# Late rows of batches 4 to 7 computed between the output tiles, in a sliding-window attention and spectral-mixing kernel on Trainium2

## The chip, the cores and the metric

One NeuronCore of a Trainium2 chip runs the whole program. The metric is the device time of one execution in microseconds (us), as the median of several executions. Profiles come from single executions taken by the hardware profiler; their time axis starts with the span. PE is TensorE (PEld its weight loads), DVE is VectorE, ACT is ScalarE, POOL is GpSimd, and SP is SyncE, which here issues all the large DMAs.

## What is computed

```python
B, H, S, D = 8, 8, 576, 64          # batch, heads, sequence, head dim; DM = H * D = 512
scores = q @ k^T / sqrt(D) - slope[h] * |i - j|       # only 0 <= i - j < 128
x = softmax(scores) @ v              # as [B, S, DM]
X = rfft(x, axis=1)[:, :64]          # 64 modes
Y[m] = X[m] @ (w_r[m] + 1j * w_i[m]) # each mode its own 512x512 complex weight
y = irfft(Y, n=S)
u = x + y
out = u + relu(u @ w_ch)             # float32, [8, 576, 512]
```

The 64 modes' weights are 134 MB in float32, and they are most of what the program reads.

## The kernel before

The program has three stages. First, attention for 32 units (batch x pair of heads). Second, a product for each pair of modes (`_modes`, L687 to L729): the weights stream from HBM into a ring in SBUF, PE multiplies, and the results collect, transposed, in `ZT`. While the weights stream, PE also prepares the output: for each of the 36 output tiles (128 rows x 512) `_xw` (L749) forms x @ w_ch, plus x itself for all tiles that are not in `RELU`, and keeps it as two bf16 halves in `hl`. Third, the end stage, `_finish` (L848), which this change is about.

What is left at the end is the inverse transform. `Z[b]` holds Y of batch b with the 128 real and imaginary mode rows on the partitions, `ZW[b]` the same times w_ch. Most rows of both are made early (`_z_early`, L768). The last 32 rows of each batch, the late rows, need the last modes, and so the last weights. `_z_late` (L799) makes them for four batches at once: 16 products (`_z_product`, L786) on PE into one PSUM bank, each giving 32 partitions (columns 32c of the array, for c = 0 to 3, and four contraction steps `et`), and one copy into a bf16 tile `zl`. There are two banks for each four batches: w = 1 is ZW (`zlw`, moving operand 512 wide, accumulated over `et`) and w = 0 is Z (`zlp`, a transpose by the identity, 128 wide). `_z_put` (L813) moves 32 rows of `zl` into Z or ZW on GpSimd, 16 moves in all.

Each output tile is a PSUM bank `u` (`_known`, L831; six banks in turn). It takes the pair of `hl` halves (L745), then ZW's part by `_taken(.., 1)` (L825), which makes it x + x @ w_ch + y @ w_ch, or without x for tiles in `RELU`. Then `_greater` (L840) forms max(u, x) on DVE (L845), or for tiles in `RELU` relu(u) on ACT (L843). Next, `_taken(.., 0)` adds y. Tiles in `RELU` also get x by one more pair of matmuls just before that. At last ACT copies the bank to SBUF (L881) and SP issues the store (L886 for whole tiles, L889 as two halves for the four tiles that hold the last 64 rows of two batches: 8, 17, 26 and 31). Each of these terms is a pair of matmuls, one for each 64-column half of the array. With h = x @ w_ch + y @ w_ch, max(x + h, x) + y and relu(h) + x + y are the same value, x + y + relu((x + y) @ w_ch).

The order in the program is written out by hand, and each engine runs its instructions in that order. Before: both banks of batches 0 to 3 (L858, L859), the ZW bank of batches 4 to 7 (L860), then the first five tiles' late terms and their max (L861 to L863), with the Z bank of batches 4 to 7 behind tile 1 (L865), all 16 puts (L866 to L870), and then the loop over tiles (L871): the last term of tile i, the start of tile i+4, the copy of tile i, the max of tile i+4, and the store of tile i. So a max is asked for four tiles ahead of the tile's last term. Output buffers (`o`) are 16.

Of the kernel before, what the change touches and what calls it, by code (L numbers as in the profile page):

```python
# [9 lines left out]
FP32 = mybir.dt.float32  # L10
BF16 = mybir.dt.bfloat16
# [5 lines left out]
P = 128  # L17
# [15 lines left out]
FT_ROWS = (2, 3, 4, 5, 6)  # L33
FT_ORDERS = (10, 14, 18, 22)
WCH_ROWS = (1, 4)
RELU = (8, 16, 24, 32)
LAST = (0, 3, 5, 6)


# [5 lines left out]
def kernel(  # L45
# [52 lines left out]
    with tc.manual_schedule(engines={ET.SP, ET.PE, ET.Activation, ET.DVE, ET.Pool}):  # L98
        with ExitStack() as wctx:
# [129 lines left out]
            for m0, w in rest_w:  # L229
# [4 lines left out]
                if done in KNOWN_AT:  # L234
# [3 lines left out]
                    known = KNOWN_AT[done]  # L238
            mctx.close()
        _finish(g)  # L240


# [499 lines left out]
def _pair(nc, out, lhsT, rhs, **kw):  # L742

    for h in range(2):
        nc.tensor.matmul(  # L745
            out[64 * h : 64 * h + 64], lhsT=lhsT[h], rhs=rhs[h], tile_position=(0, 64 * h), **kw)


def _xw(g, n, xT, psum):  # L749
# [4 lines left out]
    xw = psum.tile([P, g.DM], FP32, tag="xw", bufs=2, name="xw")  # L754
    if n not in RELU:
        nc.tensor.matmul(xw, lhsT=g.ident_b, rhs=x, start=True, stop=False)
    for dt in range(4):
        nc.tensor.matmul(  # L758
            xw, lhsT=xT[:, dt], rhs=g.wch[:, dt],
            start=(dt == 0 and n in RELU), stop=(dt == 3))  # L760
    for h in range(2):
# [24 lines left out]
def _z_product(g, ps, w, et, k, l):  # L786

    ks = slice(32 * k, 32 * k + 32)
    if w:
        g.nc.tensor.matmul(  # L790
            ps[ks], lhsT=l, rhs=g.wch[:, et], start=(et == 0), stop=(et == 3),
            tile_position=(0, 32 * k))
    else:
        g.nc.tensor.matmul(
            ps[ks, et], lhsT=l, rhs=g.ident_b, start=True, stop=True,
            tile_position=(0, 32 * k))


def _z_late(g, b0, w, pool, tag, copy):  # L799


    ps = g.eps.tile([P, 4, P], FP32, tag="zp", name="zlp") if w == 0 else (
        pool.tile([P, g.DM], FP32, tag=tag, name="zlw"))
    for et in range(4):
        for c in range(4):
            l = g.ZT[:, et, 3].rearrange("p a m b -> p (a m) b")[:, :, b0 + c]
            _z_product(g, ps, w, et, c, l)
    t = g.fin.tile([P, g.DM], BF16, tag=f"zl{w}", bufs=2, name=f"zl{w}")
    copy(t, ps if w else ps.rearrange("p a b -> p (a b)"))
    g.late[w, b0] = t  # L810


def _z_put(g, w, b):  # L813

    ks = slice(32 * (b % 4), 32 * (b % 4) + 32)
    g.nc.gpsimd.tensor_copy((g.Z, g.ZW)[w][b][ks], g.late[w, b // 4 * 4][ks])


def _taken(g, i, w, late=None):

    rows = slice(0, 32) if late else slice(0, P)
    for h, (b, s) in enumerate(g.seq[i][1]):
        o = slice(32 * (b % 4), 32 * (b % 4) + 32) if late else rows
        z = late if late else (g.Z, g.ZW)[w][b]
        g.nc.tensor.matmul(  # L825
            g.u[i][64 * h : 64 * h + 64], lhsT=g.FT[o, b % 4, s : s + 64], rhs=z[o],
            start=False, stop=(w == 0 or late is not None or i >= KNOWN),
            tile_position=(o.start, 64 * h), skip_group_check=(w == 0))


def _known(g, i):  # L831

    pool, tag = ((g.fps, "f0"), (g.fps, "f1"), (g.lps, "l0"), (g.lps, "l1"), (g.lps, "l2"),
                 (g.kps, "k0"))[i % 6]
    g.u[i] = pool.tile([P, g.DM], FP32, tag=tag, name="u")
    _pair(g.nc, g.u[i], [g.ident2] * 2, [g.hl[:, i, h] for h in range(2)],
          start=True, stop=False)


def _greater(g, i):  # L840

    if i in RELU:
        g.nc.scalar.activation(g.u[i], g.u[i], AF.Relu)  # L843
    else:
        g.nc.vector.tensor_tensor(out=g.u[i], in0=g.u[i], in1=g.seq[i][0], op=ALU.max)  # L845


def _finish(g):  # L848

    nc, tc = g.nc, g.tc
    N = len(g.seq)
    with ExitStack() as fctx:
        g.fin = pool = fctx.enter_context(tc.tile_pool(name="fin", bufs=16))
        g.kps = fctx.enter_context(
            tc.tile_pool(name="kps", bufs=1, space=bass.MemoryType.PSUM, side="right"))
        _z_late(g, 0, 1, g.eps, "zwp", nc.scalar.copy)  # L858
        _z_late(g, 0, 0, g.eps, "zp", nc.vector.tensor_copy)  # L859
        _z_late(g, 4, 1, g.kps, "k0", nc.scalar.copy)  # L860
        for i in range(KNOWN):  # L861
            _taken(g, i, 1, g.late[1, 0])
            _greater(g, i)  # L863
            if i == 1:
                _z_late(g, 4, 0, g.eps, "zp", nc.scalar.copy)  # L865
        for w, b in ((0, 0), (1, 1), (0, 1), (1, 0), (1, 2), (0, 2), (1, 3), (0, 3)):  # L866
            _z_put(g, w, b)
        for b in range(4, 8):
            for w in (1, 0):
                _z_put(g, w, b)  # L870
        for i in range(N):  # L871
            x, n = g.seq[i][0], i + AHEAD
            if i in RELU:
                _pair(nc, g.u[i], [g.ident_b[:, 0:64], g.ident_b[:, 64:128]], [x] * 2,
                      start=False, stop=True, skip_group_check=True)
            _taken(g, i, 0)
            if KNOWN <= n < N:
                _known(g, n)
                _taken(g, n, 1)
            o = pool.tile([P, g.DM], FP32, tag="o", name="o")  # L880
            nc.scalar.copy(o, g.u[i])  # L881
            if KNOWN <= n < N:
                _greater(g, n)
            _, (lo, hi) = g.seq[i]
            if hi == (lo[0], lo[1] + 64):
                nc.sync.dma_start(out=g.out[lo[0], lo[1] : lo[1] + P], in_=o)  # L886
            else:
                for h, (b, s) in enumerate((lo, hi)):
                    nc.sync.dma_start(out=g.out[b, s : s + 64], in_=o[64 * h : 64 * h + 64])  # L889
# [30 lines left out]
```

## Time and profile before

| what | value |
|---|---|
| median of 3 runs | 449.3 us (448.2 to 451.52) |
| profiled execution | 450.29 us |
| its span | 448.5 us |
| mean granted TensorE clock | 0.769 of full speed; 1.00 from 391.9 to 443.1 |
| last weights in, last product of the modes | 414.2 us |
| first late product (zlw) | 414.86 us |
| first store issued | 419.55 us |
| last copy to SBUF ends | 442.27 us |
| output | 36 tiles, 40 stores, 9.44 MB |

Some groups of the end stage, 414 to 449, with count, busy us and mean ns of one:

| line, engine, what | count | busy | mean ns |
|---|---|---|---|
| L881 ACT copy o<-u 128x512 | 36 | 19.8 | 591 |
| L845 DVE max u<-u,x 128x512 | 32 | 21.0 | 697 to 700 |
| L843 ACT relu 128x512 | 4 | 2.3 | 582 |
| L816 POOL put 32x512 | 16 | 9.5 | 607 |
| L809 ACT copy zl 128x512 | 3 | 1.8 | 585 |
| L809 DVE copy zl 128x512 | 1 | 0.7 | 692 |
| L790 PE zlw 128x512 | 32 | 2.1 | 387 |
| L794 PE zlp 128x128 | 32 | 0.9 | 230 |

A row of a timeline has the start, the time that it covers, the engine, the line, the operation, out<-in, for PE the rows and columns of the array in use (128*64 is 128 rows, 64 columns), the shape, and the count of instructions merged into the row. A matmul's row covers its latency; the next matmul starts before it is over, so starts are what to compare. A table of stretches has busy us and count for each engine, the granted clock, the mean busy share of the core's 16 DMA engines, and the GB/s that they moved. For SP, a store's row is the time to issue it; its packets move later.

### The profile page before, as it was taken

To read this page: it belongs to the slowest core of one execution; us is meant where nothing else is said; L and a number is where in the kernel's file an instruction comes from. 1 tells how busy PE (TensorE), PEld (TensorE's weight loads), DVE (VectorE), ACT (ScalarE), POOL (GpSimd) and SP (SyncE) were. 2 spreads that over 40 slices of the span, in tenths; PEclk is the share of its full clock that TensorE was granted. 3 is DMA by queue.
4 is the path that set the end of the run, shared out by engine and by line. 5 is a ranking of instruction groups with operands and counts; after the bars stand their busy time and mean duration, and the time that the engine had idled before them with its cause. 6 is when DMAs were issued, how large, how long until landed. Compare 5 with 4: busy or idle time off the path is not lost.

```text
span 448.5 us, 12893 instructions
## 1 busy us (share of the span) xinstructions
PE 294.1 (66%) x5506; PEld 204.2 (46%) x5527; DVE 216.1 (48%) x427; ACT 189.6 (42%) x302; POOL 139.1 (31%) x257
## 2 busy tenths in 40 slices
PE   2467989887787885222235664854856748696993
PEld 2455767666666763111123333432433334464661
DVE  8458566566765661010002543453535345462882
ACT  3787656584866741000011331322313233251794
POOL 7699889586876702020000000000000000000700
PEclk9969576686988975555555988589778587899997
DMA  8999999999999999999999999999999999996498
GB/s 249 346 335 327 388 325 353 347 390 379 392 368 375 393 415 429 432 425 426 430 427 433 426 429 429 427 430 426 430 429 430 426 429 430 427 428 282 185 374 288
DMA packets 51562, 173.86 MB, mean 388 GB/s; under 512 B 4912, under 2 KB 21296, under 8 KB 43440
## 3 DMA queue, kind: packets, MB, share of 16 engines
q1 hardware_dynamic: 51120, 171.99, 97.2%
q0 software_dynamic: 384, 1.05, 0.9%
q8 instruction: 43, 0.70, 0.6%
q14 instruction: 15, 0.12, 0.1%
HBM read 163.58 MB, written 9.44 MB: 386 GB/s over the span
## 4 chain that ended last, share of the span: by engine, by line
DMA 50%; PE 26%; ACT 10%; DVE 6%; issue 4%; POOL 2%; ACTq 0%; POOLq 0%
DMA ring<-in_moe_w_r_dram 47%; ACT att L459 6%; PE acc L704 5%; PE sc L447 4%; PE xt L539 4%; PE u L825 3%; PE av L493 3%; DMA ring<-in_moe_w_i_dram 3%; ACT qkT L428 3%; PE tqk L420 2%; PE u L745 2%; POOL qkb L397 1%; PE xw L758 1%; DVE x_sb L507 1%; ACT mask L311 1%
## 5 line engine op out<-in xcount | busy, mean ns | idle before, releaser
L704 PE MATMUL acc<-Xz,ring 128*128 128x32 bf16 x2048 | 70.7, 183 | 100.2 <-DMA ring<-in_moe_w_r_dram 51.0
L704 PEld LDWEIGHTS <-ring 128*128 128x128 bf16 x2048 | 61.3, 101 | 130.1 <-DMA ring<-in_moe_w_r_dram 65.1
L763 ACT CAST hl<-xw 64x512 bf16<-64x512 f32 x72 | 41.7, 579 | 105.6 <-PE xw L758 70.9
L459 ACT ACTIVATE att<-sc 128x1024 bf16<-128x1024 f32 x64 | 65.6, 1025 | 32.8 <-PE sc L447 26.7
L764 DVE TENSOR_TENSOR hl<-xw,hl 64x512 bf16<-64x512 f32 x72 | 49.6, 688 | 58.1 <-ACT hl L763 57.8
L409 POOL CAST vb<-v 64x256 bf16<-64x256 f32 x128 | 64.7, 505 | 20.1 <-PE av L493 13.7
L783 POOL MEMSET ZTa<- 32x512 bf16 x2 | 1.0, 515 | 187.5 <-ACT ZTa L781 187.5
L447 PE MATMUL sc<-qkT,qkT 64*64 64x256 bf16 (+1 forms) x512 | 32.4, 330 | 30.1 <-ACT qkT L428 16.3
L758 PE MATMUL xw<-wch,xT 128*128 128x512 bf16 x138 | 46.3, 467 | 2.7 <-issue 2.2
L428 ACT COPY qkT<-tqk 128x576 bf16<-128x576 bf16 x64 | 40.7, 638 | 0.6 <-PE tqk L420 0.6
L420 PE MATMUL tqk<-ident_b,qkb 64*64 64x64 bf16 x1152 | 31.7, 214 | 7.6 <-POOL qkb L397 6.9
L420 PEld LDWEIGHTS <-qkb 64*64 64x64 bf16 x1152 | 30.8, 130 | 10.2 <-POOL qkb L397 9.2
L464 DVE TENSOR_TENSOR att<-att,mask 128x1024 bf16<-128x1024 bf16 x32 | 26.9, 839 | 14.7 <-ACT att L459 14.5
L585 ACT ACTIVATE Xz<-xz 128x192 bf16<-128x192 f32 (+1 forms) x24 | 7.5, 313 | 59.0 <-DVE Xz L584 57.9
L493 PE MATMUL av<-vb,att 128*128 128x65 bf16 (+1 forms) x512 | 30.8, 215 | 0.6 <-issue 0.2
L584 DVE CAST Xz<-xz 128x384 bf16<-128x384 f32 (+1 forms) x24 | 12.0, 511 | 36.4 <-PE xz L578 35.7
L447 PEld LDWEIGHTS <-qkT 64*64 64x64 bf16 x512 | 13.1, 120 | 35.3 <-ACT qkT L428 18.8
L397 POOL CAST qkb<-k 128x576 bf16<-128x576 f32 x32 | 27.5, 859 | 0.0
L493 PEld LDWEIGHTS <-att 128*128 128x128 bf16 (+1 forms) x512 | 24.4, 111 | 6.5 <-issue 0.6
L397 POOL CAST qkb<-q 128x576 bf16<-128x576 f32 x32 | 24.6, 768 | 6.1 <-PE tqk L420 3.3
L738 DVE COPY xT<-tp 128x512 bf16<-128x512 bf16 x36 | 15.2, 421 | 21.9 <-PE tp L736 21.4
L469 DVE TENSOR_TENSOR att<-att,mask 128x1024 bf16<-128x1024 bf16 x32 | 25.0, 780 | 1.5 <-ACT att L459 1.1
(104 smaller groups left out, 395.2 us busy)
## 6 DMA issues: line engine op xcount, KB each, us to landing
ring<-in_moe_w_r_dram SPq DMA_DIRECT2D x32, 1536.0 KB, 13.8
ring<-in_moe_w_i_dram SPq DMA_DIRECT2D x31, 1536.0 KB, 13.7
ring<-in_moe_w_i_dram SPq DMA_DIRECT2D x33, 512.0 KB, 8.0
ring<-in_moe_w_r_dram SPq DMA_DIRECT2D x32, 512.0 KB, 7.4
q<-in_q_dram SPq DMA_DIRECT2D x32, 288.0 KB, 6.3
k<-in_k_dram SPq DMA_DIRECT2D x32, 288.0 KB, 6.2
v<-in_v_dram SPq DMA_DIRECT2D x64, 128.0 KB, 5.8
out_dram<-o SPq DMA_DIRECT2D x32, 256.0 KB, 3.3
```

Source lines behind the costliest of these rows:

```text
L397: g.nc.gpsimd.tensor_copy(tb, t)
L409: g.nc.gpsimd.tensor_copy(o[64 * r : 64 * r + 64, i], v[64 * i : 64 * i + 64, r])
L420: g.nc.tensor.transpose(tp[hs, r, :], u.b[w][hs, r], g.ident_b[hs, hs], tile_position=(64 * hh, 64 * hh))
L428: g.nc.scalar.copy(dst.rearrange("c (p r) -> c p r", r=g.R), u.tp[w].rearrange("c r p -> c p r"))
L447: nc.tensor.matmul(sc[64 * r : 64 * r + 64, hh, 256 * i : 256 * i + nq], lhsT=kT[hs, c * P + r : c * P + P : 2], rhs=qT[hs, c * P : c * P ...
L459: nc.scalar.activation(a, sc, AF.Exp, scale=1.0 / math.sqrt(g.D))
L464: nc.vector.tensor_tensor(out=a, in0=a, in1=m, op=ALU.mult)
L493: nc.tensor.matmul(av[o, hh, col(t)], lhsT=att[c // 2][:, hh, q0 : q0 + m], rhs=u.vb[:, 2 * c + hh, 0 : D + 1], start=(j == 0), stop=(t < ...
L704: nc.tensor.matmul(acc[:, et, :, m0 - c0 : m0 - c0 + n, :], lhsT=wt[:, a, et * P : (et + 1) * P], rhs=X[:, a, 1 - w : 3 - w, m0 % MB : m0 ...
L758: nc.tensor.matmul(xw, lhsT=xT[:, dt], rhs=g.wch[:, dt], start=(dt == 0 and n in RELU), stop=(dt == 3))
L763: nc.scalar.copy(g.hl[own, n, h], xw[own])
L764: nc.vector.tensor_tensor(out=g.hl[other, n, h], in0=xw[own], in1=g.hl[own, n, h], op=ALU.subtract)
```

## The change

The late rows of batches 4 to 7 are taken out of the front of the end stage. The ZW bank's 16 products go in four groups of four behind tiles 3, 5, 7 and 9 of the loop, and its copy, now on DVE, behind the last group. The Z bank's 16 products and its copy (DVE instead of ACT) follow behind tile 11. The puts of batches 4 to 7 follow these copies, ZW of batch 4 first. The ZW bank of batches 4 to 7 uses the bank `zwp` instead of `k0`.

The first copy, ZW of batches 0 to 3, is cut in two halves of 256 columns, one on ACT and one on DVE. The Z copy of batches 0 to 3 goes from DVE to ACT.

The tiles in `RELU` are 8, 13, 15, 24 and 32 instead of 8, 16, 24 and 32: `_xw` leaves out the x term for tiles 13 and 15 and forms it for 16, and in the end stage tiles 13 and 15 have their relu on ACT and one more pair of matmuls.

```diff
-RELU = (8, 16, 24, 32)
+RELU = (8, 13, 15, 24, 32)
+ZW_LATE = (3, 5, 7, 9)
+Z_LATE = 11
...
-def _z_late(g, b0, w, pool, tag, copy):
-    ps = g.eps.tile([P, 4, P], FP32, tag="zp", name="zlp") if w == 0 else (
-        pool.tile([P, g.DM], FP32, tag=tag, name="zlw"))
-    for et in range(4):
+def _z_late(g, b0, w, ets):
+    if ets[0] == 0:
+        g.lp = g.eps.tile([P, 4, P], FP32, tag="zp", name="zlp") if w == 0 else (
+            g.eps.tile([P, g.DM], FP32, tag="zwp", name="zlw"))
+    for et in ets:
         for c in range(4):
             l = g.ZT[:, et, 3].rearrange("p a m b -> p (a m) b")[:, :, b0 + c]
-            _z_product(g, ps, w, et, c, l)
-    t = g.fin.tile([P, g.DM], BF16, tag=f"zl{w}", bufs=2, name=f"zl{w}")
-    copy(t, ps if w else ps.rearrange("p a b -> p (a b)"))
-    g.late[w, b0] = t
+            _z_product(g, g.lp, w, et, c, l)
+
+def _z_copy(g, b0, w, *copies):
+    src = g.lp if w else g.lp.rearrange("p a b -> p (a b)")
+    g.late[w, b0] = t = g.fin.tile([P, g.DM], BF16, tag=f"zl{w}", bufs=2, name=f"zl{w}")
+    n = g.DM // len(copies)
+    for i, copy in enumerate(copies):
+        copy(t[:, i * n : (i + 1) * n], src[:, i * n : (i + 1) * n])
...
-        _z_late(g, 0, 1, g.eps, "zwp", nc.scalar.copy)
-        _z_late(g, 0, 0, g.eps, "zp", nc.vector.tensor_copy)
-        _z_late(g, 4, 1, g.kps, "k0", nc.scalar.copy)
+        _z_late(g, 0, 1, range(4))
+        _z_copy(g, 0, 1, nc.scalar.copy, nc.vector.tensor_copy)
+        _z_late(g, 0, 0, range(4))
+        _z_copy(g, 0, 0, nc.scalar.copy)
         for i in range(KNOWN):
             _taken(g, i, 1, g.late[1, 0])
             _greater(g, i)
-            if i == 1:
-                _z_late(g, 4, 0, g.eps, "zp", nc.scalar.copy)
         for w, b in ((0, 0), (1, 1), (0, 1), (1, 0), (1, 2), (0, 2), (1, 3), (0, 3)):
             _z_put(g, w, b)
-        for b in range(4, 8):
-            for w in (1, 0):
-                _z_put(g, w, b)
         for i in range(N):
...
             if KNOWN <= n < N:
                 _known(g, n)
                 _taken(g, n, 1)
+            if i in ZW_LATE:
+                _z_late(g, 4, 1, [ZW_LATE.index(i)])
+            if i == ZW_LATE[-1]:
+                _z_copy(g, 4, 1, nc.vector.tensor_copy)
+                _z_put(g, 1, 4)
+            if i == Z_LATE:
+                _z_late(g, 4, 0, range(4))
+                _z_copy(g, 4, 0, nc.vector.tensor_copy)
+                for w, b in ((0, 4), (1, 5), (0, 5), (1, 6), (0, 6), (1, 7), (0, 7)):
+                    _z_put(g, w, b)
             o = pool.tile([P, g.DM], FP32, tag="o", name="o")
             nc.scalar.copy(o, g.u[i])
```

## The prediction

> **What bounds the kernel now.** I read the page first: its chain of waits is DMA for half of the span (the weight stream), and the weights' last packet is in at about 414. All that the change touches lies behind that, so I went on to the end stage alone, 414.8 to 448.5: stretches with their busy times, the DMA queues, TensorE's timeline, SP's timeline.
>
> ```profile
> DMA 50%; PE 26%; ACT 10%; DVE 6%; issue 4%; POOL 2%; ACTq 0%; POOLq 0%
> ```
>
> The stretches of the end (PE, PEld, DVE, ACT, POOL busy, then granted clock, DMA share, GB/s):
>
> ```profile
> 420.40:424.00 3.60, 3.60 (x38) 2.32 (x35) 3.60 (x7) 3.25 (x7) 3.42 (x7) 1.00 0.86 332
> 424.00:430.00 6.00, 6.00 (x58) 3.93 (x56) 5.08 (x9) 5.47 (x10) 2.69 (x5) 1.00 1.01 376
> 430.00:436.00 6.00, 6.00 (x58) 3.96 (x56) 5.24 (x9) 5.48 (x11) 0.00 (x0) 1.00 1.02 380
> 436.00:442.30 6.30, 4.97 (x46) 2.92 (x40) 3.92 (x6) 5.78 (x12) 0.00 (x0) 1.00 1.00 361
> 442.30:446.60 4.30, 0.00 (x0) 0.00 (x0) 0.00 (x0) 0.00 (x0) 0.00 (x0) 0.59 0.94 339
> ```
>
> PE is full until 440, which tempts one to call it the bound. But the DMA engines are full too, and they go on being full for 4.3 us after every engine has stopped. The queue view over 420.4 to 447 says the same: the output alone fills 16 engines to 96%.
>
> ```profile
> DMA packets 5251, 9.47 MB, mean 356 GB/s; under 512 B 640, under 2 KB 640, under 8 KB 5248
> q1 hardware_dynamic: 5248, 9.44, 96.2%
> ```
>
> SP's last stores are issued back to back, although the copy that feeds the last of them ended at 442.27 (third column: how many):
>
> ```profile
> 441.65 0.62 ACT L881 COPY o<-u 128x512 f32<-128x512 f32 x1
> 442.27 2.02 SPq L886 DMA_DIRECT2D out_dram<-o  x4
> ```
>
> So the last stage is a queue of output packets, fed by PE. From the packet starts in the trace, tile 0's first packet is at 420.43 (its store was issued at 419.55), the last ends at 446.94, and there is no hole between. The time moves in two ways only: the queue starts earlier, or it runs dry.
>
> **Front of the end stage.** Before, the first late rows (zlw) are copied by ACT from 416.00 for 0.585 (ends 416.59), but PE starts the first late term of u only at 417.00: it is in the second zlw group until then.
>
> ```profile
> 415.78 0.41 PE L794 MATMUL zlp<-ident_b,ZT 128*32 128x128 bf16 x16
> 416.45 0.61 PE L790 MATMUL zlw<-wch,ZT 128*32 128x512 bf16 x8
> 417.00 0.62 PE L825 MATMUL u<-zl,FT 32*64 32x512 bf16 x4
> 417.54 0.47 PE L794 MATMUL zlp<-ident_b,ZT 128*32 128x128 bf16 x16
> 417.95 0.62 PE L825 MATMUL u<-zl,FT 32*64 32x512 bf16 x6
> 418.50 0.41 PE L825 MATMUL u<-ZTa,FT 128*64 128x512 bf16 x2
> ```
>
> After, that group is gone and two half copies run from 416.00. A half (128x256) on ACT lies between 0.330 (its 128x192 row, Xz) and 0.585: 0.38 by length. On DVE I take 0.42, its 128x256 row (ZT, two inputs); ends 0.29 (its 128x128 row) and 0.69. With the 0.05 from DVE's end to PE that the trace has at 414.81 to 414.86, the late terms start at 416.47 (416.43 to 416.74), 0.53 earlier. DVE's first max follows a first late term by 0.44 (417.00 to 417.44) and takes 0.70: it ends at 417.61. GpSimd's first put waits for the zlp copy, now on ACT behind the half copy: 416.38+0.585=416.97, as before (416.93), so the put still ends near 417.60. Tile 0's last term then starts at 417.66 instead of 418.50 (-0.84). Tile 1 waits for the second max, 0.61 behind the first: 418.26 instead of 418.79 (-0.53), and all later tiles hang on that. ACT's copy of tile 0, and so the first store, comes 0.84 earlier.
>
> **The 32 products put back between tiles.** A pair of u (two 128*64 matmuls) takes 0.216 of PE in a run of its like. The trace shows what a change of shape costs: 417.24 (last 32*64 pair) to 417.54 (zlp) is 0.30 instead of 0.216, zlp to the next pair is 0.40 for 16 products (0.23 in a run of equal shape, 415.78 to 416.01), and the pair after a change takes 0.24 (408.67 to 408.91). A zlw group of four, one wave of 512, therefore costs 0.31 in, 0.33 out (0.40 of a first wave, less the 0.07 by which the next one starts ahead of its end) and 0.24: 0.88, less the two pair steps 0.43 that would be there anyway, 0.45. Four of them: 1.80. The zlp group: 0.30+0.40+0.24-0.43=0.52. Sum 2.32. Lower end: four waves at 0.23 and 0.23, 1.15.
> The Trainium skill, "TensorEngine Tiling (Array Packing)", Key Properties, says that changing the tiling mode, not just the tile, drains the engine. The gaps of 0.30 above bear that out. With that rule the products cost the 2.32, without it 1.15; the rule speaks against spreading one block over five places.
>
> **Relu tiles.** One more than before: one more pair on PE, 0.216. On ACT a relu costs 0.51 (421.67 to 422.17) and spares DVE 0.70. ACT has the room: its copies follow each other in 0.48 when PE lets them (422.17, 422.65), against 0.65 a tile of PE. In the weight stream one matmul fewer runs (tiles 13 and 15 drop theirs, 16 gets it back): nothing, PE waits there for ring packets; uncovered it would be 0.2 earlier.
>
> **What is hidden.** The two late copies go from ACT (0.585 each) to DVE (0.69 each), between its maxima. DVE can start one every 0.60 and PE delivers every 0.65 or slower; a max is needed four tiles (2.6 us) later, so they cost nothing; without that cover 0.69 each. The puts of batches 4 to 7 (0.6 each on GpSimd) start near 427 and 428.6; the first term that reads one is tile 18's, near 430, and the rest follow two tiles ahead: hidden, uncovered at most 1 us. No DMA is added or moved and SP's order stays; waits added on PE are for semaphores of copies long done. The bank k0 that zlw no longer uses frees nothing that was waited for.
>
> **The sum on PE.** From tile 17 on PE, and with it the copies, run 2.32+0.22-0.53=2.0 later than before. The delay grows with the groups (behind tiles 3, 5, 7, 9, 11 and at the relu pairs): copies of tiles 4 and 5 end 0.1 earlier, tile 8 +0.8, tile 10 +1.3, tile 12 +1.8, tile 15 +2.2, tile 17 +2.0.
>
> **The sum on the queue.** What matters is whether a copy ends early enough. From copy end to first packet an empty queue needs 0.90 (tile 0: 419.53 to 420.43). Slack before is (first packet - copy end - 0.90): tile 5 0.63, tile 8 0.73, tile 10 1.11, tile 12 1.18, tile 15 1.16, tile 17 0.99, tile 24 1.17, tile 27 1.77, tile 35 2.55. Delay minus slack: tile 8 +0.05, tile 10 +0.2, tile 12 +0.6, tile 15 +1.05, tile 17 +1.04, tile 24 +0.85, tile 27 +0.25. So the queue starts 0.84 earlier, has lost that by tile 8, and runs behind the old one by 1.05 at tiles 15 to 17. Tile 17 leaves in two halves whose issue takes SP 1.27 (430.76 to 432.03); from a dry queue that adds up to 0.4. From tile 24 the slack has grown past the delay, and the queue alone sets the end. End of the queue: +1.05 to +1.45; I take +1.2, nearer to the slack than to the issue time, as SP's issues were shorter (0.36 to 0.46) while the queue was short (419.55, 420.04).
>
> The profiled execution took 450.29 (span 448.5, 1.8 around it), 1.0 above the median 449.3 of the three runs (448.2 to 451.52). Its sum is 451.5; against the median I forecast **450.5 us**, 0.3% slower. About 1% (4.5 us) is what a measurement of this kernel can tell from no change, so this is "the same" in that sense.
>
> **Rivals.**
> A. The queue hides all of PE's extra work and keeps the earlier start: -0.84, 448.5. For it: 96% busy and the 4.3 us at the end. Against: the slack of 0.6 to 1.2 in tiles 5 to 17. 15%.
> B. The switches are cheaper than read (products 1.15): PE's delay is 1.15+0.22-0.53=0.84, under the slack from tile 17 on but not at tile 15's relu; queue about 0 to +0.3: 449.5. Against: every change of shape in the trace costs 0.3 in. 13%.
> C. PE's delay comes through in full, since the queue's slack shrinks too when packets come singly and SP's issue becomes part of each tile: +2.0, 451.3. For it: SP needs 0.43 to 0.6 a store. Against: the tail, where slack is 2.5. 19%.
> D. Slower by over 1%: the granted clock falls to half within the end stage. Low windows before are 3.4 to 82 us long, in phases where PE waits for weights; one of 10 us here would cost 5 us of PE, 2.5 of it past the tail's slack, on top of +2.0: 449.3+4.5=453.8 and more. It decides from a low window of 10 us on. Against: clock 1.00 in every stretch up to 442, with PE no idler after the change. 3%.
> My forecast holds 49%, a gain of over 1% by something not seen 1%.
>
> **Range.** A to C span 448.5 to 451.3; the spread of runs (1.1 below to 2.2 above the median) applies to a median in small part: 448.3 to 451.9. Chances: faster by over 1% 0.01, within 1% 0.96, slower by over 1% 0.03.
>
> **What would show it.** First store issued near 418.7; PE gaps of 0.3 around each group of four; tile 17's copy some 2 us later than before; DMA share below 0.95 somewhere in 421 to 433, near 1.0 from 436. Wrong if the groups cost 0.25 each, if the share never dips (A), or if the queue still has holes in the last 10 us (C).

## The result and the profile after

| | before | after |
|---|---|---|
| median | 448.4 us (21 runs, 446.03 to 451.52) | 450.8 us (21 runs, 448.36 to 454.61) |
| profiled execution, span | 450.29, 448.5 | 454.19, 452.4 |
| first late product (zlw) to the end | 33.66 | 38.84 |

The ratio is 1.006 (95% interval 1.0041 to 1.0079), which is +2.7 us (1.8 to 3.5). The forecast was 450.5, +1.2. The forecast time is within 1% of the measured one, but the interval lies wholly above +1.2: terms of the sum were wrong. The two absolute times came nearer to each other than the two differences because the three runs that the forecast started from had a median 0.9 above that of the 21.

The start of the end stage moves by some us from one execution to the next (410.1 to 414.9 in the profiles below). So all times marked "rel" are us after the start of the first zlw product of the same execution, and "the stage" is the time from there to the end of the span.

The profiled execution of the changed kernel is 3.4 above its own median, so it probably holds something that most executions hold less of or not at all. The chain of waits of the whole span does not show it:

```profile
DMA 51%; PE 25%; ACT 9%; DVE 7%; issue 4%; POOL 2%; ACTq 0%; POOLq 0%
```

The end stage in stretches does (PE, PEld, DVE, ACT, POOL busy, then granted clock, DMA share, GB/s):

```profile
412.20:415.60 3.40, 2.00 (x46) 1.48 (x49) 0.72 (x2) 0.86 (x2) 0.00 (x0) 1.00 0.02 8
415.60:422.40 6.80, 6.80 (x34) 2.47 (x33) 4.89 (x8) 2.24 (x4) 4.70 (x8) 0.50 0.30 116
422.40:430.00 7.60, 7.60 (x84) 3.40 (x82) 4.52 (x8) 5.92 (x11) 0.60 (x1) 1.00 0.63 219
430.00:436.00 6.00, 6.00 (x58) 3.17 (x56) 5.53 (x9) 4.98 (x10) 4.10 (x7) 1.00 0.93 350
436.00:442.30 6.30, 6.30 (x62) 3.38 (x58) 5.08 (x8) 5.80 (x12) 0.00 (x0) 1.00 0.98 352
442.30:446.30 4.00, 2.56 (x22) 1.21 (x18) 2.00 (x3) 3.57 (x8) 0.00 (x0) 1.00 0.96 336
446.30:450.50 4.20, 0.00 (x0) 0.00 (x0) 0.00 (x0) 0.00 (x0) 0.00 (x0) 0.90 0.91 327
```

Two things are to be seen. In the second stretch the granted clock is 0.50: PE is busy all the time and gets through 34 matmuls (60 in `filler`, below, in a stretch of the same length at full clock). And the DMA share is 0.30 there (0.39 in a like stretch of `before_again`, below), then 0.63, and near 1 only from 436 on; before, it was 0.86 from 420.4 and 1.01 from 424 on. The queue over the output shows the same, 82.7% where it was 96.2%:

```profile
DMA packets 5252, 9.49 MB, mean 301 GB/s; under 512 B 640, under 2 KB 640, under 8 KB 5248
...
q1 hardware_dynamic: 5248, 9.44, 82.7%
```

The front of the stage, in time order (start, duration):

```profile
414.46 0.41 PE L796 MATMUL zlp<-ident_b,ZT 128*32 128x128 bf16 x16
...
414.69 0.37 ACT L818 CAST zl<-zlw 128x256 bf16<-128x256 f32 x1 [6.46 <-PE zlw L792]
...
414.96 0.59 ACT L818 CAST zl<-zlp 128x512 bf16<-128x512 f32 x1
415.09 0.42 DVE L818 CAST zl<-zlw 128x256 bf16<-128x256 f32 x1 [1.60 <-ACT zl L818]
415.57 1.06 PE L833 MATMUL u<-zl,FT 32*64 32x512 bf16 x6 [0.69 <-DVE zl L818]
```

The two halves of the first copy do not run side by side. DVE starts at 415.09, 0.03 after ACT's half is over (414.69+0.37), and the bracket says that it waited for ACT's write of the same tile. The halves share the bank that they read as well; which of the two makes them follow each other, no run here tells. Two halves one after the other take 0.83, the whole copy took 0.585. PE stands idle for 0.69, and the first late term starts at rel 2.03 instead of 2.13, a gain of 0.1.

One group of zlw products between two tiles, PE alone:

```profile
423.51 0.38 PE L833 MATMUL u<-ZTa,FT 128*64 128x512 bf16 x2
423.82 0.44 PE L792 MATMUL zlw<-wch,ZT 128*32 128x512 bf16 x4
424.19 0.41 PE L833 MATMUL u<-ZTa,FT 128*64 128x512 bf16 x2
424.43 0.38 PE L747 MATMUL u<-hl,ident 128*64 128x512 bf16 x2
```

From start to start 0.31 into the group, 0.37 out of it, 0.24 for the pair behind: 0.92 for what would be 0.43 without it. The group costs 0.49 (0.45 was forecast). The Trainium skill, "TensorEngine Tiling (Array Packing)", Key Properties, says that a change of the tiling mode drains the engine; these steps agree with that, and the experiment `wide` below takes the change of mode away.

The store of a tile for which SP is free, here tile 12, ACT's copy and SP's issue:

```profile
430.25 0.58 ACT L895 COPY o<-u 128x512 f32<-128x512 f32 x1
...
430.86 0.33 SPq L900 DMA_DIRECT2D out_dram<-o  x1
```

SP issues 0.03 after the copy ends, and by the packet starts the first packet follows at 431.90, 1.07 behind the copy's end, since tile 11's packets still move until then. At tiles 13 to 16 SP is free as well and the first packet comes 0.86 to 0.94 behind the copy's end: the queue is dry there and follows PE tile by tile. At the end it is backed up as before:

```profile
444.11 2.05 ACT L895 COPY o<-u 128x512 f32<-128x512 f32 x4 [0.29 <-PE u L833]
...
446.05 2.03 SPq L900 DMA_DIRECT2D out_dram<-o  x4
```

The last copy ends at 446.16 and the last packet at 450.81, 4.65 behind it. Before, that was 442.27 and 446.94, 4.67. So, counted from the first zlw product, the end of the queue came as much later as the last copy did.

### The profile page after: what moved, and what is told of

The parts are those of the page before. It is cut to its first block, busy times and chain, and to the rows that moved or that the text cites. A ratio compares the mean times of both kernels' runs of the same rounds, so it can differ in the third digit from the quotient of the medians.

```text
span 452.4 us, 12896 instructions
## 1 busy us (share of the span) xinstructions
PE 302.6 (67%) x5507; PEld 205.3 (45%) x5528; DVE 216.8 (48%) x428; ACT 189.9 (42%) x302; POOL 138.7 (31%) x257
## 3 DMA queue, kind: packets, MB, share of 16 engines
q1 hardware_dynamic: 51120, 171.99, 96.2%
q0 software_dynamic: 384, 1.05, 1.0%
## 4 chain that ended last, share of the span: by engine, by line
DMA 51%; PE 25%; ACT 9%; DVE 7%; issue 4%; POOL 2%; ACTq 0%; POOLq 0%
DMA ring<-in_moe_w_r_dram 46%; ACT att L461 5%; PE acc L706 4%; PE sc L449 4%; PE u L833 4%; PE xt L541 3%; DMA ring<-in_moe_w_i_dram 3%; PE av L495 3%; ACT qkT L430 2%; PE tqk L422 2%; DMA vt<-in_v_dram 2%; PE u L747 2%; DVE att L466 1%; DVE x_sb L509 1%; ACT mask L313 1%
## 5 line engine op out<-in xcount | busy, mean ns | idle before, releaser
L411 POOL CAST vb<-v 64x256 bf16<-64x256 f32 x128 | 62.3, 487 | 20.7 <-PE av L495 13.0
L449 PE MATMUL sc<-qkT,qkT 64*64 64x256 bf16 (+1 forms) x512 | 33.8, 341 | 25.5 <-ACT qkT L430 15.2
L422 PE MATMUL tqk<-ident_b,qkb 64*64 64x64 bf16 x1152 | 32.8, 220 | 7.3 <-POOL qkb L399 7.0
L422 PEld LDWEIGHTS <-qkb 64*64 64x64 bf16 x1152 | 32.5, 136 | 9.6 <-POOL qkb L399 8.9
L466 DVE TENSOR_TENSOR att<-att,mask 128x1024 bf16<-128x1024 bf16 x32 | 28.3, 886 | 13.5 <-ACT att L461 13.2
L495 PE MATMUL av<-vb,att 128*128 128x65 bf16 (+1 forms) x512 | 32.2, 220 | 0.9 <-DVE att L471 0.7
L495 PEld LDWEIGHTS <-att 128*128 128x128 bf16 (+1 forms) x512 | 25.6, 115 | 7.2 <-DVE att L471 1.1
L399 POOL CAST qkb<-q 128x576 bf16<-128x576 f32 x32 | 25.8, 805 | 5.9 <-PE tqk L422 3.0
L760 PEld LDWEIGHTS <-xT 128*128 128x128 bf16 x144 | 16.8, 118 | 19.3 <-issue 12.3
```

The source lines that it names most:

```text
L399: g.nc.gpsimd.tensor_copy(tb, t)
L411: g.nc.gpsimd.tensor_copy(o[64 * r : 64 * r + 64, i], v[64 * i : 64 * i + 64, r])
L422: g.nc.tensor.transpose(tp[hs, r, :], u.b[w][hs, r], g.ident_b[hs, hs], tile_position=(64 * hh, 64 * hh))
L449: nc.tensor.matmul(sc[64 * r : 64 * r + 64, hh, 256 * i : 256 * i + nq], lhsT=kT[hs, c * P + r : c * P + P : 2], rhs=qT[hs, c * P : c * P ...
L466: nc.vector.tensor_tensor(out=a, in0=a, in1=m, op=ALU.mult)
L495: nc.tensor.matmul(av[o, hh, col(t)], lhsT=att[c // 2][:, hh, q0 : q0 + m], rhs=u.vb[:, 2 * c + hh, 0 : D + 1], start=(j == 0), stop=(t < ...
```

## The experiments

The theories have the letters of the recorded expectations; the prediction's rivals A to D are another list. Theory S (switches): PE's added work, the products with their changes of shape, is the loss and comes through, because the queue follows PE. Theory C (clock): the low clock is a consequence of the change, and is the loss. Theory H (halves): the two half copies run in series. Against S stands the prediction's own slack account, by which the queue absorbs 0.8 of PE's delay. The edits are against the changed kernel unless another is named. The table has one profile each; first term, last copy (its end) and stage are rel, "trail" is the last packet behind the end of the last copy, "low" the stretch with a granted clock of half speed in the first 10 us.

| kernel | first term | first store | last copy | trail | stage | low | ratio (95%) |
|---|---|---|---|---|---|---|---|
| before | 2.13 | 4.69 | 27.41 | 4.67 | 33.66 | none | |
| before_again | 2.13 | 4.69 | 27.40 | 4.75 | 33.73 | none | one time, 448.22 |
| split_only | 2.13 | 4.68 | 27.40 | 5.88 | 34.83 | none | 1.0012 (0.9988 to 1.0036) |
| after | 2.03 | 5.16 | 32.62 | 4.65 | 38.84 | 6.83 | 1.006 (1.0041 to 1.0079) |
| again | 2.03 | 5.16 | 32.46 | 4.61 | 38.65 | 6.83 | one time, 451.48 |
| whole_copy | 1.78 | 4.03 | 29.77 | 5.22 | 36.56 | none | 1.0058 (1.0034 to 1.0082) |
| one_group | 2.02 | 5.16 | 31.66 | 4.31 | 37.53 | 6.83 | 1.0055 (1.0038 to 1.0072) |
| filler | 2.13 | 4.39 | 30.12 | 4.48 | 36.14 | none | 1.0054 (1.0027 to 1.0082) |
| wide | 2.02 | 4.28 | 30.28 | 4.94 | 36.76 | 3.41 | 1.0043 (1.002 to 1.0065) |
| whole_relu4 | 1.78 | 4.91 | 32.13 | 4.64 | 38.44 | 6.83 | 1.0027 (0.9998 to 1.0056) |
| wide_whole_relu4 | 1.78 | 4.03 | 28.52 | 4.59 | 34.76 | none | 1.001 (0.9978 to 1.0042) |
| left_out | 2.02 | 4.27 | 29.19 | 4.85 | 35.62 | 3.41 | 1.0022 (0.9997 to 1.0047) |
| wide_filler | 2.13 | 4.39 | 29.17 | 4.55 | 35.28 | none | 1.0031 (1.0009 to 1.0052) |
| wide_late | 1.78 | 4.03 | 28.47 | 4.54 | 34.67 | none | 1.0026 (1.0004 to 1.0048) |

**again**: the changed kernel, not altered, for a second profile.

> The changed kernel once more, unaltered, for a second profile. I measure the end stage as the span less the start of the first late product (zlw): 33.7 us before (448.5 - 414.86), 38.9 after (452.4 - 413.54). In that profile the granted clock is 0.5 from 415.57 to 422.40, which costs PE about half of 6.8 us. Theory S (switches: the 32 products put between the tiles cost PE 2.3 us with their changes of shape, and the queue of stores runs dry): a profile without the low window has an end stage of 35.2 to 35.9, 1.5 to 2.2 over before. Theory C (clock: the idle gap of PE before the first late terms, 0.9 us from start to start, brings the low window in nearly every execution, and that is the whole loss): the window is there again between 413 and 423, and the stage is 38 to 39.

Once more 6.83 us at half clock, from rel 1.66 on:

```profile
412.70:419.60 6.90, 6.51 (x34) 2.49 (x33) 4.91 (x9) 2.61 (x5) 4.70 (x8) 0.51 0.30 114
```

So the low clock is not a chance of one execution, and the stage of 38.65 is what theory C expected of a profile with the window. It took 451.48, 0.7 above the median of the changed kernel.

**whole_copy**: the first copy whole on ACT, the Z copy on DVE, as before the change.

```diff
-        _z_copy(g, 0, 1, nc.scalar.copy, nc.vector.tensor_copy)
+        _z_copy(g, 0, 1, nc.scalar.copy)
         _z_late(g, 0, 0, range(4))
-        _z_copy(g, 0, 0, nc.scalar.copy)
+        _z_copy(g, 0, 0, nc.vector.tensor_copy)
```

> The changed kernel with the first ZW copy whole again on ACT, and the Z copy of batches 0 to 3 on DVE. Theory H (halves: the DVE half started only when the ACT half had ended, 415.06 to 415.09, so the two take 0.83 us in place of 0.585): from the first zlw product to the first late term of u 1.80 us in place of 2.02, the end stage 0.2 shorter than the changed kernel's without a low window, ratio to before 0.0005 lower. If the two halves overlapped and the gap came from elsewhere: 0.2 longer.

```profile
414.15 0.58 ACT L818 CAST zl<-zlw 128x512 bf16<-128x512 f32 x1 [6.41 <-PE zlw L792]
...
414.78 1.05 PE L833 MATMUL u<-zl,FT 32*64 32x512 bf16 x10 [0.45 <-ACT zl L818]
```

The whole copy ends 0.58 after its start and the first term comes at rel 1.78, 0.25 ahead of the halves. Theory H stands. In the stretches of this profile (same columns as above) the clock stays up:

```profile
413.00:416.40 3.40, 2.79 (x44) 1.55 (x45) 1.87 (x3) 0.58 (x1) 1.21 (x3) 1.00 0.01 2
416.40:423.20 6.80, 6.63 (x60) 3.19 (x61) 5.76 (x10) 5.10 (x9) 3.49 (x6) 1.00 0.61 230
```

With the clock up and the front 0.35 earlier than before, the last copy is still 2.36 late: products and fifth relu tile cost 2.36+0.35 = 2.7 of PE. The median did not come down with the better front (1.0058 against 1.006), and 0.25 is below what these intervals can tell.

**split_only**: the kernel before, with the halves on ACT and DVE and the Z copy on ACT, and nothing else.

```diff
-        _z_late(g, 0, 1, g.eps, "zwp", nc.scalar.copy)
-        _z_late(g, 0, 0, g.eps, "zp", nc.vector.tensor_copy)
+        _z_late(g, 0, 1, g.eps, "zwp", (nc.scalar.copy, nc.vector.tensor_copy))
+        _z_late(g, 0, 0, g.eps, "zp", nc.scalar.copy)
```

> The kernel before with the split of the first copy alone (halves on ACT and DVE, Z copy of batches 0 to 3 on ACT). Both theories of the halves: the DVE half ends 0.83 us behind the start of the ACT half, when PE is still in the second zlw group, so the first late terms start where they did (2.13 us behind the first zlw product): end stage 33.5 to 33.9, ratio 0.9985 to 1.0015. Theory C: no gap on PE, no low window.

```profile
411.99 0.37 ACT L811 CAST zl<-zlw 128x256 bf16<-128x256 f32 x1 [6.64 <-PE zlw L790]
...
412.40 0.42 DVE L812 CAST zl<-zlw 128x256 bf16<-128x256 f32 x1 [1.60 <-ACT zl L811]
...
412.98 0.62 PE L830 MATMUL u<-zl,FT 32*64 32x512 bf16 x4
```

The same series, but PE is in the second zlw group meanwhile: first term at 2.13 and every copy where it was, and no difference that the times can tell. The stage of this profile is still 1.2 longer, all of it behind the last copy. Most of it comes from one store: SP took 2.24 to issue that of tile 22, whose packets then started 0.75 later than before, while those of tile 21 had still been level.

```profile
430.05 2.24 SPq L891 DMA_DIRECT2D out_dram<-o  x1
```

A difference of 1 us between the stages of two single profiles therefore proves nothing; differences of the copies do.

**one_group**: all 16 zlw products of batches 4 to 7 behind tile 9.

```diff
-            if i in ZW_LATE:
-                _z_late(g, 4, 1, [ZW_LATE.index(i)])
             if i == ZW_LATE[-1]:
+                _z_late(g, 4, 1, range(4))
                 _z_copy(g, 4, 1, nc.vector.tensor_copy)
```

> The changed kernel with all 16 zlw products of batches 4 to 7 in one run behind tile 9, none behind tiles 3, 5 and 7. Theory S: two changes of shape in place of eight, 1.10 us of PE in place of 1.80, and no delay up to tile 9: end stage 0.6 to 1.0 shorter than the changed kernel's without a low window (34.4 to 35.2), ratio to before 1.002 to 1.004. If changes of shape cost nothing on PE (four waves at 0.23 either way): no shorter than 0.3. Theory C: no difference, a low window as often as before it.

```profile
413.00:419.90 6.90, 6.50 (x34) 2.73 (x35) 4.91 (x9) 2.62 (x5) 4.70 (x8) 0.51 0.30 114
```

Again 6.83 us at half clock, so it compares with `after` and `again`: its last copy is 0.8 to 0.96 earlier. Three changes of shape in and out are worth that, some 0.3 each. The ratio was expected at 1.002 to 1.004 and did not move by an amount that its interval can tell.

**filler**: 16 more zlw products at the front, into the bank k0, which nobody reads. They keep PE as busy there as it was before the change; the products between the tiles stay.

```diff
         _z_copy(g, 0, 0, nc.scalar.copy)
+        fill = g.kps.tile([P, g.DM], FP32, tag="k0", name="fill")
+        for et in range(4):
+            for c in range(4):
+                l = g.ZT[:, et, 3].rearrange("p a m b -> p (a m) b")[:, :, 4 + c]
+                _z_product(g, fill, 1, et, c, l)
```

> The changed kernel with 16 more zlw products behind the first zlp group, into the bank k0, where nobody reads them: they fill PE's idle time before the first late terms, and cost 0.1 us there at most (2.13 from the first zlw product to the first late term, as in the kernel before, against 2.02). Theory C: no low window between 413 and 423, time near that of before (ratio 1.000 to 1.003). Theory S: ratio 1.005 to 1.008, as the changed kernel; end stage 35.3 to 36.0 where the clock stays up.

```profile
411.40:414.90 3.50, 3.27 (x60) 1.80 (x61) 1.29 (x4) 0.86 (x2) 1.30 (x3) 1.00 0.01 2
414.90:421.70 6.80, 6.61 (x60) 3.05 (x62) 5.86 (x10) 5.10 (x9) 3.40 (x6) 1.00 0.58 218
```

More work on PE, and the stage is 2.7 shorter than in `after`: the clock stays at 1.00 and the second stretch gets through 60 instructions instead of 34. That is the price of the low window where it occurs, about 2.5 us (last copy 30.12 against 32.62). But the ratio is as it was, 1.0054 against 1.006, where a window in every execution would make a difference of 0.0056; by the two intervals the difference is uncertain by about 0.003. So in the executions that set the medians the low window weighs little, at most some 1.8 us, and the +2.6 of `filler`, 2.62 between the medians, has another cause: its copy 35 is 2.71 later than before and its stage 2.48 longer. These agree, and that is theory S.

**wide**: the late products of batches 4 to 7 in the shape of the pairs around them, and otherwise the changed kernel. DVE lays their rows out batch after batch once, and one product takes two batches, 64 columns (8 and 8 instead of 16 and 16).

```diff
+            if b0 == 4:
+                if c % 2:
+                    continue
+                l, ks = g.ZL[:, et, 32 * c : 32 * c + 64], slice(32 * c, 32 * c + 64)
...
+                        g.lp[ks], lhsT=l, rhs=g.wch[:, et], start=(et == 0), stop=(et == 3),
+                        tile_position=(0, 32 * c))
```

> The changed kernel with the late products of batches 4 to 7 in the shape of u's own pairs: one copy on DVE lays the late rows out batch by batch, and each product takes two batches (64 columns of the array, 8 matmuls of 512 and 8 of 128 in place of 16 and 16), in the same places behind tiles 3, 5, 7, 9 and 11. Theory S: no change of shape, so a group is one more pair, 0.22, and the five cost 1.1 us of PE in place of 2.3: end stage 1.0 to 1.3 shorter than the changed kernel's (37.5 to 37.9 with a low window, 34.8 to 35.3 without), ratio to before 1.002 to 1.004. If the changes of shape are not what costs (the number of columns streamed is the same): stage as in the changed kernel within 0.3, ratio 1.005 to 1.007.

```profile
422.19 0.41 PE L846 MATMUL u<-ZTa,FT 128*64 128x512 bf16 x2
422.41 0.41 PE L813 MATMUL zlw<-wch,ZL 128*64 128x512 bf16 x2
422.62 0.41 PE L846 MATMUL u<-ZTa,FT 128*64 128x512 bf16 x2
422.84 0.41 PE L747 MATMUL u<-hl,ident 128*64 128x512 bf16 x2
```

No gap is left: 0.22 from start to start, in and out. A group of the same arithmetic costs 0.22 instead of 0.49. Its profile has one low window of 3.41, so its copies do not compare with `filler`; for that there is `wide_filler`.

**wide_filler**: `wide` with the filler.

> The wide products (u's own shape) together with the filler of 16 unread products in the front gap. Against the run filler this changes the shape alone, with the clock held up in both: theory S gives copies of tile 35 at 28.9 to 29.1 us after the first zlw product in place of 30.12, end stage 34.7 to 35.6 in place of 36.14, ratio 1.001 to 1.004. If shape does not matter: 30.1, 36.1, 1.0054.

The last row of ACT's copies, first of `filler` (first zlw at 411.48), then of `wide_filler` (411.88), both with the clock up:

```profile
439.55 2.05 ACT L900 COPY o<-u 128x512 f32<-128x512 f32 x4 [0.30 <-PE u L833]
```

```profile
439.00 2.05 ACT L917 COPY o<-u 128x512 f32<-128x512 f32 x4 [0.29 <-PE u L846]
```

The last copy ends at rel 30.12 and 29.17: the changes of shape cost 0.95. The stage follows by 0.86 and the ratio by 0.0023 (1.0 us), in line, though the two intervals overlap.

**whole_relu4**: `whole_copy` with the old relu tiles, `RELU = (8, 16, 24, 32)`.

> The kernel of the run whole_copy with the relu tiles of before (8, 16, 24, 32), the products spread as in the change. Theory S: one pair of matmuls less, 0.22, and ACT's relu at tile 16 again: last copy 0.2 earlier, end stage 36.0 to 36.4 against 36.56, ratio 1.004 to 1.006. If the fifth relu tile is what empties the queue: 1 us or more shorter.

```profile
411.00:414.30 3.30, 1.96 (x44) 1.45 (x45) 0.49 (x2) 0.44 (x1) 0.00 (x0) 1.00 0.05 16
414.30:421.20 6.90, 6.70 (x34) 2.50 (x33) 5.25 (x9) 2.39 (x5) 4.70 (x8) 0.51 0.30 114
```

The low window came here, without the halves. So it is not the gap of the halves alone that brings it. For the relu tile the profile does not compare. The ratio fell from 1.0058 to 1.0027, 1.4 us, more than the 0.2 of one pair; the intervals overlap, and a time that is partly that of the clock cannot size 0.2. The size of this term stays open beyond the 0.2 that a pair takes.

**wide_whole_relu4**: `wide`, `whole_copy` and the old relu tiles together, the version that the experiments up to there pointed to.

> The wide products, the first copy whole on ACT (Z copy on DVE), and the relu tiles of before (8, 16, 24, 32): what the theories S and H together would keep of the change. First store 4.0 us behind the first late product (4.69 before), PE 0.7 to 0.9 us behind the old one from tile 12 on, which the queue's slack covers: end stage 33.0 to 33.9 (33.66 before), ratio 0.998 to 1.001. Theory C alone (the gap before the first late terms is gone with the whole copy, the spread is harmless): the same, so this run tells only whether the queue's account adds up.

1.001 (0.9978 to 1.0042): within what can be told, the change's cost is gone, and nothing is gained. The last copy is at rel 28.52, still 1.1 behind before.

**left_out**: the changed kernel without the 32 late products of batches 4 to 7. The two copies stay and read the banks of batches 0 to 3, so the late rows of batches 4 to 7 are not computed but are those of 0 to 3.

```diff
-            if i in ZW_LATE:
-                _z_late(g, 4, 1, [ZW_LATE.index(i)])
             if i == ZW_LATE[-1]:
+                g.lp = g.banks[1]
...
             if i == Z_LATE:
-                _z_late(g, 4, 0, range(4))
+                g.lp = g.banks[0]
```

> The changed kernel without the 32 late products of batches 4 to 7: their copies, puts and waits stay, but read the banks of batches 0 to 3, so the last 32 mode rows of batches 4 to 7 are those of 0 to 3. Everything else of the change is there: the serial halves, the gap on PE, the fifth relu tile. Theory S (the products between the tiles are the loss): end stage 33.3 to 34.5 where the clock stays up, last copy 0.3 or less behind that of before (27.41 us after the first zlw product), ratio 0.997 to 1.002. Theory C (the thinner front lets the clock fall, and that is the loss): ratio still 1.004 or more. In 8 of the 10 profiles so far the rule holds that the clock falls for the next 3.41 us when PE streamed less than about 1.25 us of full-array work in the 3.41 us before; here the front is as thin as in the changed kernel, so a low window may come.

```profile
415.00:421.90 6.90, 6.11 (x40) 3.24 (x41) 5.49 (x9) 3.36 (x7) 4.70 (x8) 0.75 0.32 124
```

1.0022 against 1.006: 1.7 us of the 2.7 go with the products between the tiles. The last copy was expected within 0.3 of before and is 1.8 behind, since this profile has half a low stretch (clock 0.75 over 6.9 us). The front, with nothing between the tiles, is as thin as in `after`, and the low window came. The rest, 1.0 with an uncertainty of the same size, can be the relu pair and the clock; no run separates them.

**wide_late**: `wide_whole_relu4` with the groups behind tiles 8, 9, 10, 11 and the Z bank behind 14, where by the prediction's table the slack is larger.

> A version that could beat both: wide products, the first copy whole on ACT, the old relu tiles, and the groups later, behind tiles 8, 9, 10 and 11 and the Z group behind tile 14, where the queue of stores has more slack. First store 4.0 after the first late product (4.69 before), PE's delay against before -0.35 at tile 8, +0.5 at tile 12, +0.75 from tile 15. By the slack account of the prediction the queue gains 0.2 to 0.4: end stage 33.3 to 34.3 (33.7 and, by the last run with the old order, up to 34.8 before), ratio 0.998 to 1.001. If the queue has no such slack: ratio 1.001 to 1.003.

```profile
414.60:418.00 3.40, 2.75 (x44) 1.53 (x45) 1.92 (x4) 0.62 (x2) 1.25 (x3) 1.00 0.01 2
418.00:424.80 6.80, 6.53 (x60) 4.25 (x61) 6.64 (x12) 5.94 (x11) 3.92 (x6) 1.00 0.77 297
```

This was the best case for the slack account, and it was expected to gain. The clock stayed up and the queue had 91.5%, but the last copy ended 1.06 later than before, the trail was 4.54, the stage 1.0 longer and the ratio 1.0026 (1.0004 to 1.0048). The slack did not take 1 us of PE even there. On average the ratios of the five versions with the clock up (`whole_copy`, `filler`, `wide_filler`, `wide_late`, `wide_whole_relu4`) are 0.2 us below the delay of their last copies, where the slack account has up to 0.8; one interval alone can't tell that.

**before_again**: the kernel before, not altered, for a second profile.

> The kernel before once more, for a second profile of its end stage. The run with the split alone had the same copies as before within 0.02 and yet an end stage of 34.8, since its queue of stores took 27.7 in place of 26.5. I expect copies as in the first profile (tile 35 at 27.4), no low window, and an end stage between 33.5 and 35: how far it differs from 33.66 is what the DMA alone does to it.

```profile
414.30:421.20 6.90, 6.90 (x84) 4.01 (x78) 6.40 (x11) 5.65 (x12) 6.03 (x11) 1.00 0.39 148
```

The clock is 1.00 again, and every figure of the table is within 0.1 of the first profile.

## Why the prediction was right and where it was wrong

**Front: "the late terms start at 416.47, 0.53 earlier".** Wrong, it was 0.10. I priced each half (0.38 and 0.42; measured 0.37 and 0.42) and took for granted that they run at the same time. They write one tile from one bank, and DVE's half waited for ACT's in every profile that had both. The uncut copy would have given 0.35.

**First store 0.84 earlier.** Wrong: in `after` it came 0.47 later (rel 5.16), in the profiles with the clock up 0.3 earlier with the first term unmoved (`filler`, 4.39) and 0.66 earlier with the whole copy (4.03).

**The 32 products at 2.32, relu 0.22.** Right, a little low. A group cost 0.49 where 0.45 was taken, four of them 1.96; with the 0.52 taken for zlp and the relu pair that is 2.7, and `whole_copy` measured 2.7. Rival B, cheap changes of shape, falls: `wide` shows what a group costs without them, 0.22.

**PE's delay of 2.0 from tile 17 on.** It was 2.6 to 2.7 (2.71 at the last copy of `filler`), by the gain that the front did not give and the 0.2 of the products.

**"The queue alone sets the end", +1.05 to +1.45.** This is the step that failed. By the table of slack, the queue should have taken 0.8 of the 2.0, and the trail should then have fallen from 4.67 to about 3.9. ("From tile 24 the slack has grown past the delay" does not fit that table, which has the delay 0.85 above the slack at tile 24 and below it only at tile 35.) It is 4.48 to 4.65 in `after`, `again`, `filler`, `wide_filler`, `wide_late`, `whole_relu4` and `wide_whole_relu4`; only `one_group` has less (4.31), and the other three with a thinned front have more (4.85 to 5.22). Single trails move by more than 1 us (`split_only`), so the first packet of tile 35 is the better measure: against before it was 5.10 later in `after`, 2.59 in `filler`, 2.58 in `whole_copy`, 1.69 in `wide_filler` and 1.23 in `wide_late`, and the copy ahead of it 5.21, 2.71, 2.36, 1.76 and 1.06. PE's delay comes through in full, which is rival C; its +2.0 was small only because it inherited the 0.53. The account of an execution with the clock up is then 2.5 (products) + 0.2 (relu) - 0.1 (front) = 2.6, against a measured +2.7 (1.8 to 3.5).

Where the slack went can be followed by the packet starts. The table took 0.90 from a copy to its first packet as what every tile needs. For tile 17 that nearly held: in `after` tile 17's first packet came 0.73 less late than its copy. But a tile behind a split store needs more, since SP is still at the two halves when its copy is done. SP's issues of tile 17's halves and of tile 18 in `after`:

```profile
434.53 1.11 SPq L903 DMA_DIRECT2D out_dram<-o  x2
435.74 0.54 SPq L900 DMA_DIRECT2D out_dram<-o  x1
```

Tile 18's copy ended at 435.15, SP began its store at 435.74, and its first packet came at 436.94, 1.79 behind the copy. It is 1.76 to 1.81 in the seven profiles in which the queue was dry or nearly so at tile 17 and SP had no long issue behind it (`after`, `again`, `whole_copy`, `one_group`, `whole_relu4`, `wide_filler`, `wide_late`), and it was 2.08 before. (Tile 9, behind the split store of tile 8, is alike: 1.91 in `after`, 1.97 before.) So tile 18 had 0.3 of slack and not the 1.2 that 0.90 gives it. In `after` the two tiles' packets started 1.28 apart (435.66 to 436.94), 0.83 before the change: 0.45 was given back at one tile. I had named that as "up to 0.4" and then took a value near the other end. The remaining 0.3 went in the tiles behind, in part where SP took long for a single store: at tile 23 of `whole_copy` it took 1.78, and that tile's packets are 0.58 later than those ahead of it. I had taken SP's issues as short from two rows; the third row of the kernel before, at 420.54, is 1.25.

**Rival D, the clock.** The mechanism was in the list at 3% with "PE no idler after the change" against it. That reason was wrong: 32 products leave the first 2 us of the stage and the wait for the halves comes in, so PE is busy 1.96 of the 3.41 us ahead of the fall (up to rel 2.02); in the same 3.41 us it is busy 2.65 in `before` and in `filler`, and 2.20 in `whole_copy`. The price of a window was right in kind: 6.83 us of half clock cost about 2.5. Shown is that it occurs: in 6 of the 9 profiles in which the moved products have thinned the front, and in none of the 5 in which the second zlw group, or the filler in its place, is still there. Shown as well, by `filler` and within its interval, is that it does not set the medians. How often it occurs in timed executions is open; they carry no trace of the stage. Four of the 21 times of the changed kernel lie above 452.7, the profiled 454.19 among them, as do two of 12 of `whole_relu4` (452.95, its profiled one with a low window, and 454.97), while `again`, also with one, took 451.48.

Put together, the forecast's +1.2 lacked 0.4 for the front, 0.2 for the products and 0.8 for the queue: 2.6. The absolute 450.5 came near 450.8 by luck, because the small sample of before, 0.9 too high, made up for more than half of that.

## What to carry to other kernels

Two engines that copy the halves of one bank into the halves of one tile may do it one after the other; read the releaser of such a pair in a trace before counting on half the time. Slack measured tile by tile in a queue is only as good as the need that it is measured against: here a tile behind a split store needed twice the time of the first tile, and the slack reckoned from the first tile was not there. Move small PE work only in the shape of the work around it, and before thinning out a busy front, look at what keeps the granted clock up there.

## What the runs showed of the hardware

The clock fell in a busy engine. The low stretches are 3.41 or 6.83 us, one or two windows of 3.41, and the levels are 0.5 and 1.0. The Trainium skill, "TensorE: Matmul & The Clock Gate", Part 1, describes a free-running window of that length, two levels, and a fall after an idle window. Window and levels agree; the fall here came after windows in which PE was busy 1.96 to 2.39 of 3.41 us. A count of what a matmul streams (rows and columns of the array in use by streamed columns, with 0.216 us for a full 512) tells more than busy time: the window ahead of a fall held 1.21 to 1.24 us of full-array work in the six profiles, and the thinnest window about the start of the stage in the other eight 1.35 to 1.73. Where the window begins matters: `whole_copy` and `whole_relu4` have the same front, but the window from rel -0.94 held 1.36 in the first, and that from rel -1.73 held 1.24 in the second. A threshold it is not, by this count: over all 14 traces no window above 1.35 was followed by half clock and none below 0.95 by full clock, and between them both occur.

SP's issue of one 256 KB store took 0.33 on an empty queue and mostly 0.4 to 0.7 on a full one, but in each of these stages one to three stores, whole or half, took 1.0 to 2.2 (tile 2 of `before` 1.25, tile 23 of `whole_copy` 1.78, tile 22 of `split_only` 2.24), in kernels of both kinds. The cause was not looked for.
